# VectorE's exponential in three operations instead of four, and a table that decides which score banks it gets

## The chip, the cores and the metric

One core of one Trainium2 chip runs the kernel. The metric is the device time of one execution in microseconds; of several executions the median is given. Engines are called as the profile calls them: PE is TensorE's matmuls and PEld its weight loads, DVE is VectorE, ACT is ScalarE, POOL is GpSimd, SP is SyncE.

## The reference

Two transformer layers with shared weights, over S = 2048 rows of D = 448 values, 16 heads of 28, a hidden layer of 1792, all in bfloat16:

```
def A(x, wqkv, wo):                     # attention
    q, k, v = split(x @ wqkv)           # 16 heads of 28
    p = softmax(q @ k.T * 28 ** -0.5)
    return (p @ v) @ wo
def B(x, w1, b1, w2, b2):               # dense
    r = relu(x @ w1 + b1)
    return (r * r) @ w2 + b2
for layer in range(2):
    x = x + A(layernorm(x)); x = x + B(layernorm(x))
```

The softmax needs 2 x 16 x 2048 x 2048 exponentials: 1,048,576 for each of the 128 partitions. No maximum is subtracted; the sum of each row comes out of the product with the values, to which a column of ones is added.

## The kernel before

**A plan, not a loop.** The kernel issues its instructions in an order that a planner (class Planner, L145) works out while the program is built. Each piece of work is a generator ("stream") that yields Ops: an engine, a cost in us, what it depends on, what buffer it takes and gives back. The planner keeps a clock for each engine, always takes the Op that can start first, and among equals the stream with the smaller priority number. The engines then run their instructions in this order, so a change of any cost or rule orders all engines anew.

**Units, groups and banks.** The scores are cut into 2048 units, 1024 for each layer: one unit is 512 columns of scores, in one PSUM bank, for one head (128 keys by 256 queries, twice). s_stream (L865) lets PE compute the scores of three units into one of two PSUM buffers (`sc`, three banks each); this is a group, and there are 683. e_stream (L946) lets ACT take the exponential of a whole group in one instruction (L955) into an SBUF buffer `pt`. p_stream (L1054) multiplies the exponentials by the values (L1105). QK matmuls may be repeated to keep PE busy (L917 to L923), and heat (L1516) adds matmuls whose result nobody reads (L1531).

**Banks for DVE.** For each group s_stream asks `apart` (L821) whether DVE may take the third bank. If so, ACT's instruction covers two banks, 1024 columns, and DVE computes the third bank's exponential itself. `apart` says no in the first 15 groups and the last 60 units, when no scratch set is free (`sets_of`, two or three sets, each held from a unit's first operation to its last), when DVE's planned load over 11 us is above a limit, and by the test that the change touches: DVE's planned lead over PE's clock, plus `left`, the DVE time still to be planned for units already taken, must not be above TB = 2.2 us. If `behind(i)` (L805) says that the other work of the layer is behind a straight line, the limits are LOW = 0.95 of load and TB2 = 0.9 us instead. `done` (L802) counts that other work, at the end of each matmul tile of the output projection, the dense layers and the next layer's projections.

**DVE's exponential** (a_unit L1000 and a_rest L1021) has four operations on a bank of 128x512. The scores come as log2 of the exponential times 2^17. The first (L1011) reads PSUM, adds a bias, cuts off low values and writes int32: the upper 16 bits are the whole exponent, the lower 16 bits the fraction. The second (L1026, "power") reads the upper half as int16 and builds the bits of a power of two. The third (L1033, "square") computes (f + a) * f from the lower half f, as uint16. The fourth (L1041, "close") adds a constant, multiplies by the power and writes bfloat16. The first frees the score bank and has priority 1.6; the other three are a stream of their own with priority 8.5, which becomes 5.2 or 3.5 with age. The row work's evictions have 2.9 (EV), a row block's chain 4 to 4.8.

**Row work and its place.** Once a block of 256 rows has all its heads, `chain` (L1244) does output projection, layernorm, the two dense layers and, in layer 0, the keys, queries and values of layer 1 (L676, L672, L704). Its PSUM tiles are the two banks `mt`, and DVE evicts nearly all of them. Layer 1's scores begin with keys 0 to 9 (in tiles of 128 rows) for the first 13 passes and go on to keys 10 to 15 from unit 1284, so the keys of the last two row tiles of layer 0 are first needed at unit 1292.

Of the kernel before, what the change touches and what calls it, by code (L numbers as in the profile page):

```python
# [11 lines left out]
DT = mybir.dt  # L12
AF = mybir.ActivationFunctionType
ALU = mybir.AluOpType
P = 128
# [7 lines left out]

FRAC = 17
EXP_BIAS = -0.08179355555318127 * 2.0 ** FRAC
EXP_LOW = -56.0 * 2.0 ** FRAC
EXP_BASE = 91.0 * 2.0 ** 23 + 13573.0 * 2.0 ** 7
EXP_POLY = (4.803267716767392 * 2.0 ** 16, 14.031064225079138 * 2.0 ** 32)  # L30
OVER = 0.08
QUICK = 2
QUICK3 = 2
# [5 lines left out]
DCLK = 0.2  # L39
OWN = 2  # L40
HALF = 320
L0E = 1310
L0N = 7.2
L1E = 1900
L1N = 5.4
MARGIN = 1.5
LOW = 0.95
TURNS = 1
ENDU = 100
HOTE = 0.8  # L50
# [26 lines left out]
LEAD = 15  # L77
LAST = 690
BUSY = 0.995
TB = 2.2  # L80
TB2 = 0.9
SPAN = 11
NPT = 11
NOS = 2
# [154 lines left out]
def kernel(  # L239
# [12 lines left out]
    nc = tc.nc  # L252
# [16 lines left out]
    const = ctx.enter_context(tc.tile_pool(name="const", bufs=1))  # L269
# [13 lines left out]
    pl = Planner()  # L283
# [503 lines left out]
    units = []  # L787
# [11 lines left out]

    taken = set()  # L800
    held = [0]
    done = [0.0, 0.0]  # L802
    per = [1.6 + 7 + 5.6 + 6.0, 1.6 + 7 + 5.6]

    def behind(i):  # L805

        l = 0 if i < L0E else 1
        a, b, n = ((280, L0E, L0N), (1440, L1E, L1N))[l]
        return done[l] < (min(i, b) - a) / (b - a) * n * per[l] - MARGIN
    pending = [0]  # L810
    left = [0.0]

# [8 lines left out]
    def apart(i, now, us, soon=SOON):  # L821

        if len(units) - i < STOP or not LEAD <= len(gbuf) <= LAST:
            return None
        l, qb = passes[units[i][0]][:2]
        if sum(r.when() is not None and r.when() <= now + soon for r in sets_of(units[i])) <= (0 if soon else pending[0]):
            return None
        j = i
        if i + LAG > ends_at[units[i][0]]:
            j = ends_at[units[i][0]] + 1  # L830
            while j in taken:
                j += 1
            if j >= len(units):
                return None
            rows = {u[3] for u in us}
            js = [k for k in range(j, j + 4) if k < len(units) and k not in taken and units[k][3] not in rows]
            j = js[0] if js else j
        if passes[units[j][0]][0] != passes[us[0][0]][0]:
            return None
        if units[j][0] != us[0][0] and held[0] + 1 > min(sum(r.n for r in pd_free(units[k])) for k in (i, j)):  # L840
            return None
        if any(pl.tok.get(d) is None or pl.tok[d].end + LAT["DVE"] > now for d in needs(units[j])):
            return None
        if pl.load(SPAN, "DVE") > (LOW if behind(i) else BUSY):
            return None
        if max(0.0, pl.clock["DVE"] - now) + left[0] > (TB2 if behind(i) else TB):
            return None
        return j

# [116 lines left out]
    def pd_free(unit):  # L966

        pi, kb, r, hh = unit
        l, qb, *_ = passes[pi]
        if l == 0:  # L970
            return (R_pd[0], *(R_pd[1:5] if qb <= 6 else R_pd[3:5]))
        if len(norm_done.get((0, len(blocks[0]) - 1), ())) < G:
            return tuple(R_pd[:1])
        return tuple(R_pd[:1] + R_pd[6:]) if hidden_left[0] else tuple(R_pd[:1] + R_pd[5:])
# [8 lines left out]
            return V_sb[0][:, 8 + i, :, :].rearrange("p h r -> p (h r)")  # L983
        return hp.tile([P, QB], DT.bfloat16, name="h")[:, :]

    v_i = [const.tile([P, 512], DT.int32, name=f"v_i{k}") for k in range(2)]
    v_e = [const.tile([P, 512], DT.int32, name=f"v_e{k}") for k in range(2)]

    def set_of(res, l):

        k = R_v.index(res)
        two = lambda a: a.rearrange("p (a n) -> p a n", a=2)
        if k < 2:
            i, e = two(v_i[k][:, :]), two(v_e[k][:, :])
        else:
            keys = K_sb[1 - l][:, :, S - 512:S] if l == 0 else K_sb[0][:, :, 0:512]
            i, e = keys[:, 0:2, :].bitcast(DT.int32), keys[:, 2:4, :].bitcast(DT.int32)
        return i, e, i.bitcast(DT.float32), two

    def a_unit(gi, x, src, unit, l):  # L1000
        yield Op("-", 0.0, None, deps=[("s", gi)])
        box = {}

        def take(e):
            pending[0] -= 1
            box["i"], box["e"], box["h"], two = set_of(c.res, l)
            box["two"] = two
            halves = box["i"].bitcast(DT.uint16).rearrange("p a (n t) -> p a n t", t=2)
            box["f"] = halves[:, :, :, 0]
            box["n"] = box["i"].bitcast(DT.int16).rearrange("p a (n t) -> p a n t", t=2)[:, :, :, 1]  # L1010
            t = nc.vector.tensor_scalar(out=box["i"], in0=two(src), scalar1=EXP_BIAS,  # L1011
                                        scalar2=EXP_LOW, op0=ALU.add, op1=ALU.max)
            if x is gbuf[gi]["s"]:
                apart_from(gi, t)
        c = Op("DVE", 0.69, take, deps=[("s", gi)], acq=sets_of(unit), rel=x)
        left[0] += 2.14
        yield c
        left[0] -= 0.6
        pl.spawn(lambda now: V_LAST if e_now[1] - gi >= V_AGE or at[0] > ends_at[unit[0]] + V_PAST else V_LATE if now > c.end + V_WAIT else V_PRIO if gi > FIRST else V_FIRST, a_rest(gi, c, box, unit))

    def a_rest(gi, c, box, unit):  # L1021

        lin, low = EXP_POLY

        def power(e):
            nc.vector.tensor_scalar(out=box["e"], in0=box["n"], scalar1=2.0 ** 22, scalar2=EXP_BASE,  # L1026
                                    op0=ALU.mult, op1=ALU.add)
        p = Op("DVE", 0.42, power, deps=[c])
        yield p
        left[0] -= 0.34  # L1030

        def square(e):
            nc.vector.scalar_tensor_tensor(out=box["h"], in0=box["f"], scalar=lin, in1=box["f"],  # L1033
                                           op0=ALU.add, op1=ALU.mult)
        h = Op("DVE", 0.684, square, deps=[c, p])
        yield h
        left[0] -= 0.6

        def close(e):
            pd = gbuf[gi]["pd"] = gbuf[gi]["pt"][:, 1024:1536] if gbuf[gi]["in"] else pd_of(o)  # L1040
            nc.vector.scalar_tensor_tensor(out=box["two"](pd), in0=box["h"], scalar=low, in1=box["e"].bitcast(DT.float32),  # L1041
                                           op0=ALU.add, op1=ALU.mult)
        own = gbuf[gi]["in"]
        o = Op("DVE", 0.683, close, deps=[p, h, ("e", gi)] if own else [p, h], acq=None if own else lambda: pd_free(unit), rel=c, sets=("x", gi))
        gbuf[gi]["x"] = o
        yield o
        left[0] -= 0.6
# [196 lines left out]
    def chain(l, qb):  # L1244
# [3 lines left out]
        n = nt * P  # L1248
# [8 lines left out]
        for j in range(nt):  # L1257
            if whole:
                def both(e, t):
                    nc.vector.tensor_copy(out=x_sb[:, t0, :], in_=t[:, 0:D])  # L1260
                a = yield from mm_tile(
                    [(0, D, [(ident[:, :], x_sb[:, t0, :])] + [(oTn[:, g, 0:P], wo[:, g, :], *([("on", l, qb, g)] if end else [])) for g in range(G)])],
                    both, 0.61, [*([] if end else norm_done[l, qb]), *[("wo", i) for i in range(G)]],
                    alone=G if end else 0, seen=lambda last, t: stats(mv, t0, 0, [last], src=lambda: t()[:, 0:D]))
                done[l] += 0.8
                continue
            a = yield from mm_tile(
                [(0, D, [(oTn[:, g, j * P:(j + 1) * P], wo[:, g, :], *([("on", l, qb, g)] if end else [])) for g in range(G)])],
                add_to_x(t0 + j), 0.61, [*([] if end else norm_done[l, qb]), *[("wo", i) for i in range(G)]],
                post=[lambda a, j=j: stats(mv, t0, j, [a])], alone=G - 1 if end else 0)  # L1270
            done[l] += 0.8
        yield Op("DVE", 0.0, None, deps=[a], rel=own_on)
        xnT, own_xt, ends = yield from layernorm(t0, nt, None, mv=mv, x_in=a, parts=late > 2 - THALF)
        rows_done.add((l, qb))
# [15 lines left out]
        for f0 in range(0, NFC, pack):  # L1290
            fcs = range(f0, min(f0 + pack, NFC))
            w = len(fcs) * n
            split = late > 2 - THALF and f0 == 0
            b = {}
# [15 lines left out]
            def then(o, b=b, square=square):  # L1310
# [4 lines left out]
                [(i * n, n, [(w1[:, dc, fc * P:(fc + 1) * P], xnT[:, dc, 0:n], *([ends[dc // 2]] if split else [])) for dc in range(NDC)])  # L1315
                 for i, fc in enumerate(fcs)],
                relu, 0.685, [*([] if split else ends), ("w1",)], True, post=[then], acq=R_r, across=split)
            done[l] += w / 512
            for i in range(len(fcs)):
                hacts.append((b, i, b["s"]))  # L1320
        yield Op("DVE", 0.0, None, deps=[o], rel=own_xt)
# [1 line left out]
        for j in range(nt):  # L1323
            tb = t0 + j
            own_deps = l == 1 and qb >= len(blocks[1]) - OWN
            halves = [(0, D)] if not HALF or (l, qb) != (1, len(blocks[1]) - 1) else [(0, HALF), (HALF, D)]
            for lo, hi in halves:
                def store(e, tb=tb, lo=lo, hi=hi):
# [4 lines left out]
                    add_to_x(tb, lo, hi), 0.15 + (hi - lo) / 950, [*([] if own_deps else [hacts[-1][2]]), ("w2",), ("b2",)],  # L1333
                    post=[(lambda a, j=j: stats(mv, t0, j, [a])) if l == 0 else
                          (lambda a, store=store: [Op("DMA", 0.5, store, deps=[a])])])
            done[l] += 2.8
        yield Op("DVE", 0.0, None, deps=[a], rel=own_h)
        hidden_left[0] -= l == 0
        if l == 0:
            xt2 = yield from layernorm(t0, nt, None, mv=mv)  # L1340
            yield from qkv(1, t0, nt, *xt2)
            done[0] += 6.0

    def finish(l, qb):

# [237 lines left out]
```

## Time and profile before

| | us |
|---|---|
| median of 3 runs | 857.73 (856.56 to 859.1) |
| span of the profiled execution, first to last instruction | 854.4 |
| median less span | 3.3 |
| ACT busy | 838.1 (98%), of which exponentials 827.5 |
| PE busy | 812.8 (95%) |
| DVE busy | 809.8 (95%) |
| last exponential ends at | 840.0 |

The profiled execution is one execution, and the profile gives its span; no other time of it is recorded. The median of the timed runs is 3.3 us above that span. A line of instructions in the profile names line, engine, operation, output and inputs, shapes, how often, busy us in total, mean ns of one, and the engine's idle time ahead of it. Two instructions of one engine can overlap in the records, so that sums of durations may exceed the time they fill; the distance from one start to the next is then the better measure.

### The profile page before, as it was taken

The numbers are of one execution on the slowest core, as the hardware profiler recorded it, in microseconds if no ns is written. First come the engines' busy times: TensorE is split into PE (matmuls) and PEld (weight loads), VectorE is DVE, ScalarE is ACT, GpSimd is POOL, SyncE is SP. The second block draws the span as 40 slices with busy tenths as digits, with TensorE's granted clock in tenths as the row PEclk, the third lists the DMA queues.
The fourth block names the chain that finished last, engine by engine and source line by source line (L and its number), as shares of the span: only waits on it lengthen the run. The fifth ranks groups of instructions, "written<-read, shape, count | busy, mean of one in ns | idle before, by whom it ended". The sixth has DMA issues, their size and how long they took to land.

```text
span 854.4 us, 28129 instructions
## 1 busy us (share of the span) xinstructions
PE 812.8 (95%) x12245; PEld 431.4 (50%) x12245; DVE 809.8 (95%) x1687; ACT 838.1 (98%) x699; POOL 40.1 (5%) x94
## 2 busy tenths in 40 slices
PE   8999999999999999999999999999999999999997
PEld 4445554554545545455445444544454544545665
DVE  7999999999999999999999999999999999999965
ACT  8999999999999999999999999999999999999994
POOL 3100000001000010000000000000000000000000
PEclk9999999999999999999999999899999999999999
DMA  9200100000000000000000000011000000000000
GB/s 247 67 3 2 28 16 15 14 16 15 15 3 15 16 15 15 7 11 15 2 2 2 3 2 2 16 29 28 29 13 20 21 26 20 17 17 14 20 14 13
DMA packets 32364, 17.97 MB, mean 21 GB/s; under 512 B 17833, under 2 KB 31787, under 8 KB 32240
## 3 DMA queue, kind: packets, MB, share of 16 engines
q1 hardware_dynamic: 32240, 16.18, 6.8%
q8 instruction: 95, 1.56, 0.8%
q14 instruction: 29, 0.24, 0.1%
HBM read 13.88 MB, written 2.07 MB: 19 GB/s over the span
## 4 chain that ended last, share of the span: by engine, by line
PE 35%; ACT 32%; DVE 24%; issue 7%; DMA 0%; SPq 0%; POOL 0%; ACTq 0%; DVEq 0%
ACT pt L955 32%; PE mt L653 15%; PE sc L930 12%; PE oT L1105 6%; DVE v_i L1011 3%; DVE v_i L1033 3%; DVE pt L1041 2%; DVE r L1301 2%; DVE K_sb L1011 2%; DVE v_e L1026 2%; DVE K_sb L1033 1%; PE mt L1531 1%; DVE V_sb L1041 1%; DVE x_sb L1241 1%; DVE st L507 1%
## 5 line engine op out<-in xcount | busy, mean ns | idle before, releaser
L955 ACT ACTIVATE pt<-sc 128x1536 bf16<-128x1536 f32 (+1 forms) x683 | 827.5, 1446 | 2.5 <-PE sc L930 2.1
L930 PE MATMUL sc<-Q_sb,K_sb 32*128 32x256 bf16 (+1 forms) x5192 | 303.6, 266 | 28.3 <-ACT pt L955 24.0
L930 PEld LDWEIGHTS <-K_sb 32*128 32x128 bf16 x5192 | 128.5, 92 | 210.0 <-issue 163.2
L1105 PE MATMUL oT<-pt,V_sb 128*32 128x256 bf16 (+1 forms) x4084 | 152.5, 269 | 0.3 <-DVE Q_sb L672 0.2
L653 PE MATMUL mt<-xnT,w 128*128 128x256 bf16 (+1 forms) x888 | 118.9, 271 | 2.1 <-DVE xnT L569 0.7
L1105 PEld LDWEIGHTS <-V_sb 128*32 128x32 bf16 x4352 | 91.4, 96 | 46.5 <-issue 43.0
L1011 DVE TENSOR_SCALAR v_i<-sc 128x512 int32<-128x512 f32 x154 | 104.9, 681 | 5.6 <-PE sc L930 5.2
L1033 DVE SCALAR_TENSOR_TENSOR v_i<-v_i 128x512 f32<-128x512 uint16 x154 | 104.3, 679 | 0.5
L653 PEld LDWEIGHTS <-w 128*128 128x128 bf16 x896 | 75.0, 98 | 37.6 <-issue 28.3
L1301 DVE TENSOR_SCALAR r<-mt 128x512 bf16<-128x512 f32 x108 | 73.6, 681 | 3.8 <-PE mt L653 3.4
L653 PE MATMUL mt<-w,V_sb 128*128 128x448 bf16 (+1 forms) x288 | 70.0, 348 | 0.0
L1026 DVE TENSOR_SCALAR v_e<-v_i 128x512 int32<-128x512 int16 x154 | 62.8, 413 | 0.5
L1531 PE MATMUL mt<-xn,ident 128*128 128x448 bf16 x161 | 53.9, 358 | 2.0 <-DVE oT_sb L1133 0.4
L534 POOL TENSOR_TENSOR ve<-mv,eps_t 128x2 f32<-128x2 f32 (+1 forms) x33 | 9.4, 285 | 779.0 <-DVE mv L512 779.0
L1041 DVE SCALAR_TENSOR_TENSOR pt<-v_i,v_e 128x512 bf16<-128x512 f32 x63 | 42.9, 681 | 0.7
L1241 DVE TENSOR_TENSOR x_sb<-x_sb,mt 128x448 bf16<-128x448 bf16 x62 | 37.7, 610 | 5.5 <-PE mt L653 5.3
L1011 DVE TENSOR_SCALAR K_sb<-sc 128x512 int32<-128x512 f32 x60 | 41.0, 683 | 2.1 <-PE sc L930 1.9
L1033 DVE SCALAR_TENSOR_TENSOR K_sb<-K_sb 128x512 f32<-128x512 uint16 x60 | 40.8, 680 | 0.3
L507 DVE BATCH_NORM_STATS2 st<-x_sb 128x6 f32<-128x448 bf16 x63 | 38.7, 614 | 0.5 <-DMA x_sb<-in_A_x_dram 0.4
L1041 DVE SCALAR_TENSOR_TENSOR V_sb<-v_i,v_e 128x512 bf16<-128x512 f32 x54 | 36.7, 679 | 0.2
L653 PEld LDWEIGHTS <-V_sb 128*128 128x128 bf16 x302 | 24.1, 97 | 24.4 <-issue 11.4
L653 PE MATMUL mt<-wo,oTn 128*128 128x448 bf16 x124 | 30.7, 355 | 0.4 <-DVE oT_sb L1133 0.3
(135 smaller groups left out, 736.0 us busy)
## 6 DMA issues: line engine op xcount, KB each, us to landing
rec<-scr SPq DMA_DIRECT2D x54, 128.0 KB
x_sb<-in_A_x_dram SPq DMA_DIRECT2D x8, 224.0 KB
out_dram<-x_sb SPq DMA_DIRECT2D x15, 112.0 KB
w<-in_B_w_dram SPq DMA_DIRECT2D x1, 1568.0 KB
w<-in_B_w_dram SPq DMA_DIRECT2D x1, 1344.0 KB
dn<-oT_sb SPq DMA_DIRECT2D x54, 4.0 KB
V_sb<-in_A_wqkv_dram SPq DMA_DIRECT2D x4, 168.0 KB
scr<-dn SPq DMA_DIRECT2D x27, 8.0 KB
```

Of the source, the lines that this page charges most:

```text
L507: nc.vector.bn_stats(out=box["st"][:, :], in_=x_sb[:, t0 + j, :] if src is None else src())
L653: nc.tensor.matmul(box["t"][:, c0:c0 + n], lhsT=lhsT() if callable(lhsT) else lhsT, rhs=rhs, start=a, stop=b)
L930: nc.tensor.matmul(dst[k][:, i * nt * P:(i + 1) * nt * P], lhsT=K_sb[l][rows, g, (kb + i) * P:(kb + i + 1) * P], rhs=Q_sb[rows, g, t0 * P: ...
L955: t = nc.scalar.activation(out=pt[:, 0:n], in_=gbuf[gi]["sc"][:, 0:n], func=AF.Exp, scale=float(np.log(2.0)) * 2.0 ** -FRAC)
L1011: t = nc.vector.tensor_scalar(out=box["i"], in0=two(src), scalar1=EXP_BIAS, scalar2=EXP_LOW, op0=ALU.add, op1=ALU.max)
L1026: nc.vector.tensor_scalar(out=box["e"], in0=box["n"], scalar1=2.0 ** 22, scalar2=EXP_BASE, op0=ALU.mult, op1=ALU.add)
L1033: nc.vector.scalar_tensor_tensor(out=box["h"], in0=box["f"], scalar=lin, in1=box["f"], op0=ALU.add, op1=ALU.mult)
L1041: nc.vector.scalar_tensor_tensor(out=box["two"](pd), in0=box["h"], scalar=low, in1=box["e"].bitcast(DT.float32), op0=ALU.add, op1=ALU.mult)
L1105: nc.tensor.matmul(box["t"][DHP * hh:DHP * hh + DHP, 0:n], lhsT=V_sb[l][:, kb + i, 4 * g + hh, :], rhs=p[:, c0:c0 + n], start=begin and kb ...
L1241: nc.vector.tensor_tensor(out=x_sb[:, tb, lo:hi], in0=x_sb[:, tb, lo:hi], in1=t[:, 0:hi - lo], op=ALU.add)
L1301: nc.vector.tensor_scalar(out=r[:, 0:w], in0=t[:, 0:w], scalar1=0.0, scalar2=None, op0=ALU.max)
L1531: nc.tensor.matmul(t[:, 0:D], lhsT=ident[:, :], rhs=xns[0][:, 0:D], start=True, stop=True)
```

## The change

DVE's exponential gets three operations. Scores now come as log2 times 2^7. The first operation (tensor_scalar, PSUM to SBUF) writes float32 after an addition that puts the value where the low 16 bits of its float32 pattern hold the position within one octave. The second (scalar_tensor_tensor) reads these low halves as int16 and computes a bend, (f * c) * f, into a second float32 scratch tile. The third (scalar_tensor_tensor) adds value, constant and bend and writes the sum as int16 into the bfloat16 tile: the whole number is the bit pattern of the result. The operation "power" is gone; the scratch tile `v_e` (int32) becomes `v_h` (float32) of the same size. The planner's figure for a unit is 1.80 instead of 2.14 us.

The tests `behind`, LOW, TB and TB2 and the counting in `done` go. In their place stands PACE, 64 limits of 0.3 to 6.0 us; unit number i uses entry i * 64 // 2048, so each entry covers 32 units. The load limit is BUSY = 0.995 always.

```diff
-FRAC = 17
-EXP_BIAS = -0.08179355555318127 * 2.0 ** FRAC
-EXP_LOW = -56.0 * 2.0 ** FRAC
-EXP_BASE = 91.0 * 2.0 ** 23 + 13573.0 * 2.0 ** 7
-EXP_POLY = (4.803267716767392 * 2.0 ** 16, 14.031064225079138 * 2.0 ** 32)
+FRAC = 7
+EXP_MID = 0.506
+EXP_LOW = 128.0 * 128
+EXP_SHIFT = 184.0 * 128 - round(EXP_MID * 2.0 ** 16) / 512
+EXP_BEND = 0.3418455151161652 * 128 / 65536 ** 2
+EXP_BITS = (127.0 - 0.08538929525245402) * 128 - EXP_SHIFT
...
-TB = 2.2
-TB2 = 0.9
+PACE = (3.6, 3.6, 3.6, 1.8, 1.8, 1.8, 1.8, 1.8, 0.3, 0.9, 2.2, 2.2, 2.2, 2.6, 3.0, 3.0, 3.0, 3.6, 6.0, 2.2, 2.2, 2.2, 4.5, 2.2, 3.0, 2.6, 2.2, 2.2, 2.6, 2.6, 1.8, 1.8, 2.2, 2.6, 2.6, 1.8, 1.8, 1.8, 2.2, 2.6, 3.0, 6.0, 2.6, 4.5, 1.4, 1.4, 1.4, 1.4, 1.4, 1.4, 1.4, 1.4, 2.2, 2.2, 2.2, 2.2, 2.2, 2.2, 2.2, 2.2, 2.2, 2.2, 2.2, 2.2)
...
-        if pl.load(SPAN, "DVE") > (LOW if behind(i) else BUSY):
+        if pl.load(SPAN, "DVE") > BUSY:
             return None
-        if max(0.0, pl.clock["DVE"] - now) + left[0] > (TB2 if behind(i) else TB):
+        if max(0.0, pl.clock["DVE"] - now) + left[0] > PACE[i * len(PACE) // len(units)]:
             return None
...
-            halves = box["i"].bitcast(DT.uint16).rearrange("p a (n t) -> p a n t", t=2)
-            box["f"] = halves[:, :, :, 0]
-            box["n"] = box["i"].bitcast(DT.int16).rearrange("p a (n t) -> p a n t", t=2)[:, :, :, 1]
-            t = nc.vector.tensor_scalar(out=box["i"], in0=two(src), scalar1=EXP_BIAS,
+            box["f"] = box["i"].bitcast(DT.int16).rearrange("p a (n t) -> p a n t", t=2)[:, :, :, 0]
+            t = nc.vector.tensor_scalar(out=box["i"], in0=two(src), scalar1=EXP_SHIFT,
                                         scalar2=EXP_LOW, op0=ALU.add, op1=ALU.max)
...
-        left[0] += 2.14
+        left[0] += 1.80
...
-        def power(e):
-            nc.vector.tensor_scalar(out=box["e"], in0=box["n"], scalar1=2.0 ** 22, scalar2=EXP_BASE,
-                                    op0=ALU.mult, op1=ALU.add)
-        p = Op("DVE", 0.42, power, deps=[c])
-        yield p
-        left[0] -= 0.34
-
         def square(e):
-            nc.vector.scalar_tensor_tensor(out=box["h"], in0=box["f"], scalar=lin, in1=box["f"],
-                                           op0=ALU.add, op1=ALU.mult)
-        h = Op("DVE", 0.684, square, deps=[c, p])
+            nc.vector.scalar_tensor_tensor(out=box["h"], in0=box["f"], scalar=EXP_BEND, in1=box["f"],
+                                           op0=ALU.mult, op1=ALU.mult)
+        h = Op("DVE", 0.684, square, deps=[c])
...
-            nc.vector.scalar_tensor_tensor(out=box["two"](pd), in0=box["h"], scalar=low, in1=box["e"].bitcast(DT.float32),
-                                           op0=ALU.add, op1=ALU.mult)
+            nc.vector.scalar_tensor_tensor(out=box["two"](pd.bitcast(DT.int16)), in0=box["i"], scalar=EXP_BITS, in1=box["h"],
+                                           op0=ALU.add, op1=ALU.add)
```

## The prediction

> **What bounds the kernel now.** First the page's busy times: ACT 98%, PE and DVE 95% each. Three engines near the top say only that shares cannot decide. Second, what ACT waited for over the whole run:
>
> ```profile
> ACT pt L955 <- PE sc L930: 2.1, 5, 1.0
> ```
>
> Only 2.1 us of waiting for scores, in 5 places. Third, the same line with its two shapes kept apart, and busy times by stretch. The stretches run from the first bank that DVE takes (30.1 us) to the end of the last (807.5), and from the end of the last exponential (839.9) to the end of the span; the columns are the length, then busy time and count of PE, PEld, DVE, ACT and POOL, PE's granted clock, DMA share and GB/s:
>
> ```profile
> L955 ACT ACTIVATE pt<-sc 128x1536 bf16<-128x1536 f32 x468 | 668.7, 1581 | 1.8 <-PE sc L930 1.4
> L955 ACT ACTIVATE pt<-sc 128x1024 bf16<-128x1024 f32 x215 | 236.9, 1154 | 0.8 <-PE sc L930 0.7
> ...
> 30.10:807.50 777.40, 745.33 (x11094) 388.70 (x11092) 756.33 (x1538) 776.26 (x646) 29.25 (x67) 1.00 0.05 14
> ...
> 839.90:854.40 14.50, 10.76 (x133) 7.83 (x131) 7.54 (x26) 3.04 (x7) 0.56 (x1) 0.99 0.06 18
> ```
>
> ACT is busy 776.3 of 777.4 us: its exponentials stand end to end and set the time. 468 x 3 + 215 x 2 banks = 1834, and DVE's 214 make the 2048. DVE is idle 777.4 - 756.3 = 21.1 us of the stretch, so ACT cannot give it many more banks as things are. The kernel is bound by the two together: ACT by its exponentials, DVE by how many banks it can relieve ACT of.
>
> **What a bank is worth to ACT.** 1581 - 1154 = 427 ns. The records overlap, but the starts agree: the median distance from one exponential to the next is 1.331 us after three banks and 0.904 after two. The count of 683 instructions stays, since a group is always three units.
>
> **What a bank costs DVE now.** The four operations, in their most frequent forms:
>
> ```profile
> L1011 DVE TENSOR_SCALAR v_i<-sc 128x512 int32<-128x512 f32 x154 | 104.9, 681 | 5.6 <-PE sc L930 5.2
> L1033 DVE SCALAR_TENSOR_TENSOR v_i<-v_i 128x512 f32<-128x512 uint16 x154 | 104.3, 679 | 0.5
> ...
> L1026 DVE TENSOR_SCALAR v_e<-v_i 128x512 int32<-128x512 int16 x154 | 62.8, 413 | 0.5
> L1041 DVE SCALAR_TENSOR_TENSOR pt<-v_i,v_e 128x512 bf16<-128x512 f32 x63 | 42.9, 681 | 0.7
> ```
>
> Durations of 681 + 413 + 679 + 681 make 2.45 us, but the timeline (start, duration) shows that they are not the cost:
>
> ```profile
> 143.92 0.68 DVE L1033 SCALAR_TENSOR_TENSOR v_i<-v_i 128x512 f32<-128x512 uint16 x1
> 144.52 0.42 DVE L1026 TENSOR_SCALAR K_sb<-K_sb 128x512 int32<-128x512 int16 x1
> 144.86 0.68 DVE L1041 SCALAR_TENSOR_TENSOR pd<-v_i,v_e 128x512 bf16<-128x512 f32 x1
> 145.46 0.68 DVE L1033 SCALAR_TENSOR_TENSOR K_sb<-K_sb 128x512 f32<-128x512 uint16 x1
> ...
> 402.25 0.69 DVE L1033 SCALAR_TENSOR_TENSOR v_i<-v_i 128x512 f32<-128x512 uint16 x1
> 402.98 0.69 DVE L1041 SCALAR_TENSOR_TENSOR V_sb<-v_i,v_e 128x512 bf16<-128x512 f32 x1
> ```
>
> From start to start a long operation takes 0.60 us (144.86 to 145.46) and the power 0.34 (144.52 to 144.86). Where an operation needs the one just ahead of it, the slot grows by about 0.12 (402.25 to 402.98). A unit so takes 3 x 0.60 + 0.34 = 2.14 us.
>
> **What the change removes.** The power, 0.34 us for each unit: 214 x 0.34 = 73 us of DVE. The three that stay keep their size, and their slots should stay at 0.60. The first writes float32 instead of int32 from PSUM; L1301, which also reads a PSUM bank but writes bf16, has 681 ns as well, so the output type is not what counts. The square reads int16 instead of uint16 in the same places. The close reads two float32 tiles as before and writes int16 instead of bf16, two bytes either way. For these I take nothing; bounds from the rows are 0.34 (413 ns, the shortest operation on a bank of 512) and 0.60 + 0.12 us for each. Dependent pairs fall from three in a unit to two, and a filler between the first and the third operation goes; I take the two as equal. The change issues no DMA, adds no wait to another engine, and moves no queue but through the new plan.
>
> The Trainium skill, "VectorE: DVE Perf Modes", section "The DRAIN you can't avoid", says that the next operation does not start until the pipe of the one before is empty. Taken as a slot of the whole recorded duration, the power would be worth 0.413 us and all units 88 us, and the result by the sum below would be 842.4 before the idle time is touched; the timeline does not agree, with starts 0.08 us ahead of the recorded ends.
>
> **Where the freed time goes.** If the planner took no more banks, DVE would just idle and the time would stay, since ACT has the same work. What it takes more is decided by the tests in apart. All of them let DVE fill up: the load limit stays 0.995, the backlog test has 2.2 or more in 44 of 64 entries and counts 1.80 us for a unit instead of 2.14, and a scratch set is held for less time. So I set the balance with DVE as full as now. In the stretch, units fill 214 x 2.14 = 458.0 us; other work and idle time are 777.4 - 458.0 = 319.4. With n units the stretch is 777.4 - 0.427 (n - 214) on ACT and 319.4 + 1.80 n on DVE. Equal: 2.227 n = 549.4, n = 246.7. So 32.7 more banks, 14.0 us less. The idle 21.1 us is the other term: none of it to all of it can be filled, the latter giving n = 256.2 and 18.0 us; I take a third, because most of DVE's waits that the trace names are for PE's tiles, which stay. 7.0 us is 3.2 units and 1.3 us. **The sum is 14.0 + 1.3 = 15.3 us**, so the profiled execution of 854.4 becomes 839.1. The median lies 3.3 above that span; I keep that: 842.4.
>
> **What must hold beside it.** PE has the same useful work in 15 us less. It is busy 745.3 of 777.4, but that holds filling: L930 ran 5192 matmuls where 2048 units need 4352 (layer 1's last two blocks need four per unit), and L1531 ran 161 with 53.9 us that nobody reads. The cover is several times 15 us; gone, each us of PE would count in full. The granted clock dips once, and ACT does not notice:
>
> ```profile
> 534.00:560.70 26.70, 25.47 (x385) 12.96 (x384) 25.41 (x52) 26.43 (x24) 0.00 (x0) 0.87 0.06 13
> ```
>
> Start (10.8 us) and tail (14.5) have no bank for DVE and stay.
>
> **Rival 1: the rows of layer 0 come too late, slower.** Layer 1's scores need the last keys of layer 0's rows at unit 1292, about the 431st group, whose exponential starts near 533 us. The timeline has these keys written just in time:
>
> ```profile
> 530.24 0.68 DVE L676 CAST K_sb<-mt 128x512 bf16<-128x512 f32 x1
> 530.84 0.68 DVE L1011 TENSOR_SCALAR v_i<-sc 128x512 int32<-128x512 f32 x1
> ...
> 538.16 0.68 DVE L676 CAST K_sb<-mt 128x512 bf16<-128x512 f32 x1
> ```
>
> The progress test that held DVE for the rows (0.9 us when behind) is gone, and the table's entries ahead of that unit are 1.8 to 2.6. A bank taken there beyond the balance pushes the rows back 1.80 us and spares 0.43, a net loss of 1.37. 135 units were taken by 531 us, so 21 of the 33 new ones belong there; 14.0 / 1.37 = 10 further ones eat the gain, and 12 make it slower by 0.3%. With 15 it is 20.6 lost, 863. For it: no slack at 530 us. Against: only the first operation has a priority ahead of the rows (1.6), the other two wait at 8.5 behind evictions at 2.9. Chance 0.09.
>
> **Rival 2: score banks come free late, slower.** With more units in flight DVE's first operation may end after ACT's and hold the buffer. To lose 15.3 + 2.6 us, 250 units must each delay ACT by 72 ns; I put it at 862. Now in 206 of 214 cases the first operation ends ahead of ACT's own exponential of that group, in the median by 0.45 us. Chance 0.03.
>
> **Rival 3: the freed time is not refilled.** The table is tight (0.3 and 0.9 for units 256 to 319, 1.4 for 1408 to 1663), or a scratch set is the limit: it is held 6.0 us in the mean, 214 x 6.0 / 777 = 1.65 sets of two or three. Nothing gained is 857.7, chance 0.06 within 0.3%; a part of it, 6 to 20 banks, is 849 to 855, chance 0.12.
>
> **More than forecast:** all idle time and all 0.12 us gaps filled adds to 20.5 us, 837; below that 0.02.
>
> **How the numbers follow.** Forecast 842.4 with 837 to 849 around it: 0.68. A measurement tells about 0.3%, 2.6 us, from no change. Faster by more: 0.68 + 0.12 + 0.02 = 0.82. Same: 0.06. Slower: 0.09 + 0.03 = 0.12. The range 837 to 854 leaves out rivals 1 and 2, the standstill and a little at either end, some 0.2.
>
> **What would show it.** About 250 first and last operations on DVE and about 250 exponentials of 128x1024; slots still 0.60; ACT's wait for scores a few us; the last exponential near 825. Wrong if the count of 128x1024 stays at 215 to 225, if ACT's idle time grows around the keys of layer 0's last rows, or if a scalar_tensor_tensor with int16 in or out takes longer than 0.68 us.

## The result and the profile after

| | before | after |
|---|---|---|
| median, us | 857.29 (856.56 to 859.10, 4 runs) | 848.77 (848.31 to 848.86, 4 runs) |
| span of the profiled execution | 854.4 | 847.0 |
| ratio of the times, 95% interval | | 0.990 (0.9886 to 0.9914) |
| banks on DVE | 214 | 244 |
| first exponential starts, last one ends | 10.85, 839.96 | 10.66, 832.54 |
| last exponential's end to end of span | 14.4 | 14.4 |

The change makes the kernel 1.0% faster: 8.5 us by the medians, 7.4 by the two profiled spans. (The median before has one run more than ahead of the prediction, hence 857.29 in place of 857.73.) The forecast was 842.4, a gain of 15.3. The time lies in the range; the gain is a little over half of the forecast by the medians and a little under half by the spans.

The groups of the kernel after show what became of the four operations and of ACT's instruction (count, then busy us and mean ns of one):

```profile
L941 ACT ACTIVATE pt<-sc 128x1536 bf16<-128x1536 f32 x438 | 628.4, 1566 | 4.0 <-PE sc L916 3.6
L941 ACT ACTIVATE pt<-sc 128x1024 bf16<-128x1024 f32 x245 | 263.6, 1143 | 2.8 <-PE sc L916 2.6
```

The DVE groups of the kernel after, first operation, square and close:

```profile
L995 DVE TENSOR_SCALAR v_i<-sc 128x512 f32<-128x512 f32 x175 | 119.1, 682 | 6.9 <-PE sc L916 6.1
L1008 DVE SCALAR_TENSOR_TENSOR v_h<-v_i 128x512 f32<-128x512 int16 x175 | 117.5, 679 | 0.5
...
L995 DVE TENSOR_SCALAR K_sb<-sc 128x512 f32<-128x512 f32 x69 | 47.1, 683 | 3.1 <-PE sc L916 2.4
...
L1016 DVE SCALAR_TENSOR_TENSOR pt<-v_i,v_h 128x512 int16<-128x512 f32 x64 | 43.0, 672 | 0.3
```

The three operations cost what their forerunners did, 672 to 683 ns, with int16 in or out; from one start to the next each has a median of 0.60 us, as before. 175 + 69 = 244 units went to DVE, 30 more, and the three-bank exponentials fell from 468 to 438. That alone is worth 30 x 0.427 = 12.8 us. ACT's waits in the kernel after show where a part of it went:

```profile
ACT pt L941 <- PE sc L916: 6.2, 11, 2.2
```

6.2 us where it was 2.1. Measured from start to start, against 1.331 us after three banks and 0.904 after two, ACT's excess over back-to-back is 17.1 us; before it was 11.4. The spans add up: 0.2 from an earlier start, 12.8 from the banks, 5.7 given back, the tail the same: 7.3 of the 7.4.

Two places hold most of the 5.7, 4.8 together. Between 30 and 110 us the excess rose from 1.05 to 4.12, between 545 and 560 us from 0.97 to 2.69. The first is a row-work deadline of layer 0: its last keys (row tiles 12 to 15) are first needed at units 160 and 164. ACT in the kernel after around it (start, duration, and the idle time ahead in brackets):

```profile
74.36 4.91 ACT L941 ACTIVATE pt<-sc 128x1536 bf16<-128x1536 f32 x4
81.51 1.02 ACT L941 ACTIVATE pt<-sc 128x1024 bf16<-128x1024 f32 x1 [2.24 <-PE sc L916]
```

DVE in the same stretch of the kernel after:

```profile
77.54 0.68 DVE L1008 SCALAR_TENSOR_TENSOR v_h<-v_i 128x512 f32<-128x512 int16 x1
78.14 0.68 DVE L563 COPY xnT<-tp 128x1024 bf16<-128x1024 bf16 x1
78.74 0.68 DVE L1016 SCALAR_TENSOR_TENSOR V_sb<-v_i,v_h 128x512 int16<-128x512 f32 x1
79.34 0.41 DVE L1108 TENSOR_TENSOR K_sb<-oT,K_sb 128x256 f32<-128x256 f32 x1
79.67 0.68 DVE L1008 SCALAR_TENSOR_TENSOR v_h<-v_i 128x512 f32<-128x512 int16 x1
80.27 0.68 DVE L670 CAST K_sb<-mt 128x512 bf16<-128x512 f32 x1
```

ACT stands still for 2.24 us because the scores wait for the keys that L670 writes at 80.27; DVE has no gap, and three of the five operations ahead belong to banks that it took (L1008, L1016). The same keys were written earlier in the kernel before:

```profile
76.66 0.69 DVE L676 CAST K_sb<-mt 128x512 bf16<-128x512 f32 x1 [0.47 <-PE mt L653]
```

The keys of the same rows for the other heads follow at 86 us with 0.8 us more. The second place is a stretch of half granted clock, taken up under fill.

DVE's stretch in the kernel after, with the columns of the prediction's table:

```profile
30.10:800.00 769.90, 741.43 (x11094) 388.06 (x11095) 739.47 (x1413) 764.14 (x646) 30.82 (x66) 0.99 0.05 14
```

DVE's idle time there is 769.9 - 739.5 = 30.4 us; it was 21.1. So DVE was not filled further, as the forecast assumed, but a little less.

### The profile page after: what moved, and what is told of

It reads as the page before. It is cut to its first block, busy times and chain, and to the rows that moved or that the text cites. A ratio compares the mean times of both kernels' runs of the same rounds, so it can differ in the third digit from the quotient of the medians.

```text
span 847.0 us, 27977 instructions
## 1 busy us (share of the span) xinstructions
PE 809.2 (96%) x12200; PEld 430.6 (51%) x12200; DVE 793.7 (94%) x1563; ACT 826.4 (98%) x699; POOL 41.7 (5%) x94
## 4 chain that ended last, share of the span: by engine, by line
PE 48%; ACT 27%; DVE 15%; issue 7%; DMA 2%; POOL 1%; ACTq 0%; SPq 0%; DVEq 0%
ACT pt L941 27%; PE mt L647 20%; PE sc L916 16%; PE oT L1080 8%; DVE v_i L995 2%; DVE v_h L1008 2%; PE mt L1501 2%; DVE r L1274 1%; DVE pt L1016 1%; DVE K_sb L1008 1%; DVE K_sb L995 1%; DVE st L501 1%; DVE x_sb L1216 1%; DMA rec<-scr 1%; DVE xn L611 1%
## 5 line engine op out<-in xcount | busy, mean ns | idle before, releaser
L941 ACT ACTIVATE pt<-sc 128x1536 bf16<-128x1536 f32 (+1 forms) x683 | 815.7, 1415 | 6.8 <-PE sc L916 6.2
L916 PE MATMUL sc<-Q_sb,K_sb 32*128 32x256 bf16 (+1 forms) x5180 | 306.8, 267 | 27.6 <-ACT pt L941 21.5
L916 PEld LDWEIGHTS <-K_sb 32*128 32x128 bf16 x5180 | 131.6, 92 | 205.9 <-issue 153.1
L1080 PE MATMUL oT<-pt,V_sb 128*32 128x256 bf16 (+1 forms) x4034 | 154.5, 270 | 0.7 <-DVE pt L1016 0.3
L995 DVE TENSOR_SCALAR v_i<-sc 128x512 f32<-128x512 f32 x175 | 119.1, 682 | 6.9 <-PE sc L916 6.1
L1008 DVE SCALAR_TENSOR_TENSOR v_h<-v_i 128x512 f32<-128x512 int16 x175 | 117.5, 679 | 0.5
L1080 PEld LDWEIGHTS <-V_sb 128*32 128x32 bf16 x4352 | 90.9, 96 | 50.0 <-issue 46.9
L1274 DVE TENSOR_SCALAR r<-mt 128x512 bf16<-128x512 f32 x108 | 73.4, 680 | 4.7 <-PE mt L647 4.4
L995 DVE TENSOR_SCALAR K_sb<-sc 128x512 f32<-128x512 f32 x69 | 47.1, 683 | 3.1 <-PE sc L916 2.4
L1008 DVE SCALAR_TENSOR_TENSOR K_sb<-K_sb 128x512 f32<-128x512 int16 x69 | 46.8, 678 | 0.3
L1216 DVE TENSOR_TENSOR x_sb<-x_sb,mt 128x448 bf16<-128x448 bf16 x62 | 37.6, 611 | 7.3 <-PE mt L647 6.8
L1501 PE MATMUL mt<-xn,ident 128*128 128x448 bf16 x128 | 44.1, 357 | 0.3
L1016 DVE SCALAR_TENSOR_TENSOR pt<-v_i,v_h 128x512 int16<-128x512 f32 x64 | 43.0, 672 | 0.3
L1016 DVE SCALAR_TENSOR_TENSOR V_sb<-v_i,v_h 128x512 int16<-128x512 f32 x63 | 42.5, 678 | 0.2
L647 PEld LDWEIGHTS <-wk 128*128 128x128 bf16 x256 | 22.2, 97 | 11.4 <-issue 8.3
```

Of the source, the lines that this page charges most:

```text
L647: nc.tensor.matmul(box["t"][:, c0:c0 + n], lhsT=lhsT() if callable(lhsT) else lhsT, rhs=rhs, start=a, stop=b)
L916: nc.tensor.matmul(dst[k][:, i * nt * P:(i + 1) * nt * P], lhsT=K_sb[l][rows, g, (kb + i) * P:(kb + i + 1) * P], rhs=Q_sb[rows, g, t0 * P: ...
L941: t = nc.scalar.activation(out=pt[:, 0:n], in_=gbuf[gi]["sc"][:, 0:n], func=AF.Exp, scale=float(np.log(2.0)) * 2.0 ** -FRAC)
L1016: nc.vector.scalar_tensor_tensor(out=box["two"](pd.bitcast(DT.int16)), in0=box["i"], scalar=EXP_BITS, in1=box["h"], op0=ALU.add, op1=ALU.add)
L1080: nc.tensor.matmul(box["t"][DHP * hh:DHP * hh + DHP, 0:n], lhsT=V_sb[l][:, kb + i, 4 * g + hh, :], rhs=p[:, c0:c0 + n], start=begin and kb ...
L1216: nc.vector.tensor_tensor(out=x_sb[:, tb, lo:hi], in0=x_sb[:, tb, lo:hi], in1=t[:, 0:hi - lo], op=ALU.add)
```

## The experiments

Theory 1: ACT's exponentials stand end to end and set the time; a bank on DVE is worth 0.427 us of it, and each wait of ACT for scores counts in full. Cheaper banks let DVE take more, but the table's part is that keys are written by the time they fall due. Theory 2, the rival: DVE is the bound, and what is saved for each bank shows whatever the order. Times are medians, with the ratio to the kernel before on the same chip and its 95% interval.

**ops_only**: the new operations with the old limits.

```diff
-        if pl.load(SPAN, "DVE") > BUSY:
+        if pl.load(SPAN, "DVE") > (LOW if behind(i) else BUSY):
...
-        if max(0.0, pl.clock["DVE"] - now) + left[0] > PACE[i * len(PACE) // len(units)]:
+        if max(0.0, pl.clock["DVE"] - now) + left[0] > (TB2 if behind(i) else TB):
```

> The three operations with the old limits (behind, LOW, TB, TB2) in place of the table. Theory 1 (ScalarE's exponentials stand end to end and set the time; a bank given to VectorE is worth 0.427 us, and every wait of ScalarE for scores counts in full; the table's part is that the last keys of a layer are written before their scores are due): the planner's own order here has 243 banks on VectorE, so 29 x 0.427 = 12.4 us less of exponentials than before, but a wait for scores of some 7 us at the keys of layer 0's last rows (unit 1292, near 525 us) and of some 3 us near 78 us, and more work left after the last exponential: 856 to 862, no gain. Theory 2 (VectorE is the bound, so its time saved per bank shows whatever the order): 847 to 851, like the changed kernel.

Measured: 862.05, ratio 1.0058 (1.0039 to 1.0078), 243 banks. With one bank fewer than the changed kernel it is 0.6% slower than before. ACT at the due keys in ops_only:

```profile
525.10 3.84 ACT L956 ACTIVATE pt<-sc 128x1024 bf16<-128x1024 f32 x3
536.79 5.54 ACT L956 ACTIVATE pt<-sc 128x1024 bf16<-128x1024 f32 x5 [7.85 <-PE sc L931]
```

DVE's cast of these keys in ops_only:

```profile
535.00 0.69 DVE L677 CAST K_sb<-mt 128x512 bf16<-128x512 f32 x1 [1.96 <-PE mt L654]
```

The keys due near 527 us came at 535.0, and ACT waited 7.85 us. The time after the last exponential grew too, to 18.8 us. The time is at the upper edge of theory 1's range and 11 us above that of theory 2.

**table_only**: the four operations with the table (the same two lines the other way round, in the kernel before).

> The four operations of before with the table in place of the old limits. Theory 1: 213 banks, so the same exponentials as before, plus waits of some 5 us at unit 1292 that the old limits did not have: 861 to 867, slower than before. Theory 2: VectorE's work is that of before, 855 to 859. A table that is good by itself: below 855.

Measured: 869.63, 1.0144 (1.0116 to 1.0173), 213 banks; the wait at the due keys is 6.2 us. It lies 2.6 us above the range of theory 1: other waits came on top (12.2 us in all), with a half clock of 20.5 us after 556 us. The table is no gain by itself.

**cap214**: the changed kernel, banks held to the old number.

```diff
+        if len(taken) >= (i - 45) * 214 / 1945:
+            return None
```

> The changed kernel, but the number of banks for VectorE is held to a straight line that ends at 214, as many as before. Theory 1: VectorE's freed time is idle, ScalarE has the exponentials of before: 855 to 861, no gain although every bank costs VectorE less. Theory 2: 214 x 0.34 = 73 us less of VectorE's work show at least in part: below 852.

Measured: 858.75, 1.0017 (1.0005 to 1.0029). The stretch of before, 30.1 to 807.5 us (length, then PE, PEld, DVE, ACT, POOL), in cap214:

```profile
30.10:807.50 777.40, 745.15 (x11180) 395.37 (x11181) 702.95 (x1324) 774.75 (x645) 31.81 (x66) 1.00 0.05 14
```

DVE is busy 703.0 us where it was 756.3, and the time is that of before within 0.3%. 53 us taken from an engine that is 97% busy bought nothing, as long as no bank moved. (53 and not 73: an operation that nothing follows at once counts with its whole 0.68 instead of 0.60, and DVE's gaps rose from 138 to 321, which is worth some 15 us of the 20.)

**flat22**: all 64 entries 2.2.

```diff
-PACE = (3.6, 3.6, 3.6, 1.8, ...
+PACE = (2.2,) * 64
```

> The changed kernel with all 64 entries of the table 2.2, the old general limit, and nothing that looks at progress. Theory 1: 242 banks (12.0 us less of exponentials), but the rows of layer 0 come late: a wait of some 7 us near 525 us, one of some 10 us close to the end, and the 3 us near 78 us: 864 to 870, slower than before with 28 more banks on VectorE. Theory 2: 847 to 851.

Measured: 868.69, 1.0151 (1.0124 to 1.0177), 242 banks. ACT at the due keys in flat22:

```profile
537.05 4.40 ACT L941 ACTIVATE pt<-sc 128x1024 bf16<-128x1024 f32 x4 [8.49 <-PE sc L916]
```

There are three long waits of ACT, near the places that theory 1 named: 2.6 us near 79 us by the starts, 8.5 at the due keys and 9.1 near 833 us. The last is not a wait for keys: ACT waits there until PE has multiplied earlier exponentials by the values (L1080), behind matmuls of the dense layers. 28 more banks than before, and 1.5% slower.

**flat22_hold**: flat22 with five entries changed.

```diff
-PACE = (2.2,) * 64
+PACE = (2.2,) * 36 + (0.3,) * 5 + (2.2,) * 23
```

> The table is 2.2 everywhere, as in flat22, but its entries 36 to 40 (units 1152 to 1311, about 470 to 537 us, just ahead of and around the unit that needs the last keys of layer 0's rows) are 0.3. Theory 1 (what matters is that the rows' keys are written in time): 239 banks, three fewer than flat22, and yet 852 to 858, some 12 us faster than flat22's 868.7, with no wait of ScalarE over 1 us between 500 and 545 us. Theory 2 (more banks, more gain): flat22's time or 1 us more, 868 to 871.

Measured: 858.22, 1.0005 (0.9993 to 1.0017), 239 banks. By the medians it is 10.5 us faster than flat22, with three banks fewer. The casts of the last keys in flat22_hold:

```profile
525.12 0.68 DVE L670 CAST K_sb<-mt 128x512 bf16<-128x512 f32 x1
532.28 0.68 DVE L670 CAST K_sb<-mt 128x512 bf16<-128x512 f32 x1
```

They come in time, and there is no wait over 1 us there. The time is 0.2 us above theory 1's range. Its span is 9.4 us longer than the changed kernel's: 4.1 at the end (18.5 us after the last exponential instead of 14.4), 2.1 from five banks fewer, and 3.4 from more excess of ACT, of which 2.1 fall between 541 and 562 us, where the clock is halved for 20.5 us.

**keys_earlier**: the same work, the keys due 20 units earlier.

```diff
-AHEAD = (range(0, 4), range(0, 4), range(0, 4), range(0, 1))
+AHEAD = (range(0, 4), range(0, 4), range(0, 4), range(0, 0))
```

> The changed kernel with its table, but layer 1's first cut has 12 passes instead of 13 (AHEAD's last entry empty), so that the last keys of layer 0's rows are needed 20 units, some 8 us, earlier; the amount of work is the same. Theory 1: 248 banks, four more, but a wait of 5 to 8 us near 520 us where the changed kernel has none, and a longer end: 855 to 861. Theory 2: 846 to 849.

Measured: 860.28, 1.0039 (1.0024 to 1.0054), 248 banks. ACT in keys_earlier:

```profile
514.80 6.12 ACT L941 ACTIVATE pt<-sc 128x1536 bf16<-128x1536 f32 x5
528.22 1.94 ACT L941 ACTIVATE pt<-sc 128x1024 bf16<-128x1024 f32 x2 [7.30 <-PE sc L916]
```

DVE's cast of the due keys, first in keys_earlier, then in the changed kernel:

```profile
526.12 0.69 DVE L670 CAST K_sb<-mt 128x512 bf16<-128x512 f32 x1 [1.96 <-PE mt L647]
...
526.90 0.69 DVE L670 CAST K_sb<-mt 128x512 bf16<-128x512 f32 x1 [1.19 <-PE mt L647]
```

The keys are written at almost the same time; the due date moved by 8 us, and a wait of 7.3 us comes where there was none. In the changed kernel the keys end at 527.6 us and ACT's exponential that needs them starts at 528.2: they have next to no room.

**no_load_limit**: the limit on DVE's planned load lifted.

```diff
-BUSY = 0.995
+BUSY = 9.0
```

> The changed kernel without the limit of 0.995 on VectorE's planned load over 11 us (set to 9). Theory 1: 259 banks, 15 more, 6.4 us less of exponentials, but there is no room for them: the last keys of layer 0's rows come some 25 us late and the end is longer: 872 to 882, the slowest with the most banks. Theory 2: 840 to 845.

Measured: 881.14, 1.0292 (1.0271 to 1.0313). The two shapes of the exponential in no_load_limit:

```profile
L941 ACT ACTIVATE pt<-sc 128x1536 bf16<-128x1536 f32 x423 | 616.8, 1583 | 3.4 <-PE sc L916 2.9
L941 ACT ACTIVATE pt<-sc 128x1024 bf16<-128x1024 f32 x260 | 287.0, 1148 | 33.7 <-PE sc L916 33.5
```

ACT at the due keys in no_load_limit:

```profile
524.92 2.98 ACT L941 ACTIVATE pt<-sc 128x1536 bf16<-128x1536 f32 x2
552.70 1.94 ACT L941 ACTIVATE pt<-sc 128x1024 bf16<-128x1024 f32 x2 [24.80 <-PE sc L916]
```

259 banks, the least exponential time of all, and the slowest kernel. This also shows that with this table it is the load limit that keeps the number of banks at 244. With that limit, the kernels with three operations have 237 to 248 banks with every table tried here, cap214 aside.

**late_start**: DVE's first bank at group 40.

```diff
-LEAD = 15
+LEAD = 40
```

> The changed kernel, but VectorE gets its first bank at group 40 instead of 15 (LEAD), so that the opening's keys are not behind it. Theory 1: 237 banks, 7 fewer, 3.0 us more of exponentials; the wait of 3.4 us at 78 and 86 us is gone; the sum is 847 to 850, the same as the changed kernel's 848.8. Theory 2: 3 us slower, 851 to 853.

Measured: 850.14, 0.992 (0.9903 to 0.9937), 237 banks. No wait near 79 us is left, and the span of the profiled execution, 847.5, equals that of the changed kernel within 0.5 us with seven banks fewer. The median is just above the range of theory 1; two of the four runs had more half clock.

**fill**: more for PE around 548 us, where the clock is halved.

```diff
-                for i in list(range(4)) * (again + 1):
+                for i in list(range(4)) * (again + 1 + (438 <= gi < 462)):
```

> The changed kernel in the same order, but the score matmuls of groups 438 to 461 (about 540 to 565 us) are issued once more, so that TensorE does more there. In the changed kernel the granted clock is 0.5 for 10.2 us from 547.9 us, and ScalarE's excess over back-to-back between 545 and 560 us is 2.7 us. Theory A (TensorE does too little just ahead, the clock falls, and the scores then come late): the stretch of 0.5 gets shorter or goes, the excess there falls below 1 us, 846 to 848. Theory B (the waits there come from the order of the work, the clock has no part): the excess stays or grows by the added matmuls, 849 to 851.

Measured: 854.54, 0.9968 (0.9953 to 0.9984), from 850.3 to 857.4: slower than the changed kernel and above the ranges of both theories. The half clock did not go; it scattered. Sorted by mean granted clock, the spans of the 12 runs are 848.5 at 1.000, 850.1 to 850.2 at 0.996, 852.6 to 852.8 at 0.992, 854.2 to 854.3 at 0.990 and 855.5 to 855.6 at 0.988. So the time goes with the clock, some 1.2 us of span for each 3.4 us of half clock. But the added matmuls cost by themselves: the run at 1.000 is 1.5 us longer than the changed kernel's 847.0 at 0.994. And they kept the clock up in only one run of the 12.

**late_start2**: first bank at group 35, and one entry of the table.

```diff
-LEAD = 15
+LEAD = 35
...
-PACE = (..., 2.6, 2.6, 1.8, 1.8, 2.2, ...     # entries 28 to 32
+PACE = (..., 2.6, 2.6, 4.5, 1.8, 2.2, ...
```

> The changed kernel with VectorE's first bank at group 35 instead of 15, and entry 30 of the table (units 960 to 991) 4.5 instead of 1.8. Theory 1: 239 banks, 5 fewer, 2.1 us more of exponentials; the wait of 3.4 us of the opening is gone, all else as in the changed kernel: 847 to 848.5, about 1 us faster than it. Theory 2: 2 us slower, 850 to 852.

Measured: 847.61, 0.989 (0.9875 to 0.9905), 239 banks. Its waits for scores:

```profile
ACT pt L941 <- PE sc L916: 3.1, 8, 0.6
```

The opening's wait is gone, for 2.1 us more of exponentials. It has the lowest time of all, by 1.2 us in the medians; its interval overlaps that of the changed kernel (0.9886 to 0.9914), so that it is better is not shown.

**both**: late_start2 with the matmuls of fill.

> late_start2 with the added matmuls of fill. Theory 1 with theory A: both gains, 845 to 847.5. If the clock has no part: as late_start2, 847 to 850.

Measured: 850.82, 0.9936 (0.9916 to 0.9957), above the ranges of both theories. Here the profiled execution has no half clock in the stretch. Busy times and clock from 520 to 560 us in late_start2, which has the same order without the added matmuls (length, PE, PEld, DVE, ACT, POOL, clock, DMA share, GB/s):

```profile
520.00:560.00 40.00, 37.90 (x555) 19.76 (x554) 35.67 (x67) 38.36 (x34) 0.97 (x3) 0.87 0.07 17
```

The same stretch in both:

```profile
520.00:560.00 40.00, 38.32 (x668) 22.39 (x667) 35.49 (x67) 38.35 (x33) 0.86 (x3) 1.00 0.07 17
```

ACT is busy 38.4 of 40 us in each: here a full clock with added matmuls leaves as much waiting as 10.2 us of half clock without them. Over the 12 runs of both the span is 846.3 to 846.6 at a clock of 1.000 and 854.0 to 854.5 at 0.988. Whether the dip could be kept away without that price stays open.

## Why the prediction was right or wrong

**What bounds the kernel** was right. cap214 shows it for DVE: 53 us cheaper, no bank moved, no gain. For ACT it is the sum of the spans above, which comes out within 0.1 us from the count of banks and ACT's waits. PE's condition held too: in the kernel after, filling is left, with 5180 matmuls in L916 where 4352 are needed and 44.1 us in L1501 that nobody reads.

**The value of a bank, 0.427 us,** and **its cost on DVE, three slots of 0.60 us**, held, and int16 in or out cost nothing more, as taken. A slot of the whole recorded duration, which the prediction sets beside this, did not come; the passage of the Trainium skill that it cites for it ("VectorE: DVE Perf Modes", section "The DRAIN you can't avoid") itself adds that a next operation that is not held starts earlier.

**The balance** was a little high: 247 banks with DVE as full as before, 250 with a third of its idle time filled. It came to 244, with 9 us more idle. The step that failed is the one that took "a third, because most of DVE's waits that the trace names are for PE's tiles, which stay". They grew: DVE's waits that end with PE went from 13.5 to 22.3 us in its stretch. 6 banks fewer are 2.5 us of the 7.9 us by which the span missed. (The prediction lets the stretch before end with DVE's last bank at 807.5 us; that bank ends at 816.2, but DVE is not idle in between, so the 21.1 us stay.)

**The waits of ACT** are the larger miss. The forecast had no term for them: it expected "a few us" as before, and the 5.7 us more are the rest. Rival 1 had the place and the sign: ops_only, flat22, keys_earlier and no_load_limit wait 7.3 to 24.8 us for the keys that it named. But it was priced as a mishap at one place, and it showed at a second one where scores need keys that DVE evicts: at layer 0's own keys (units 160 to 180) the changed kernel pays 3.4 us of it by the starts. "Start and tail have no bank for DVE and stay" was true of the groups ahead of DVE's first bank and hid this. Its arithmetic, that 15 banks beyond the balance ahead of the due keys lose 20.6 us net, was too mild: no_load_limit has 15 more than after, 10 of them ahead of these keys, and is 32 us slower. Nor is it the number of banks alone. By 510 us DVE has begun 147 banks in the changed kernel, and 147 in flat22 and ops_only as well. Yet of the eleven results of the dense layers that DVE evicts between 440 and 530 us (L1274 in after and flat22, L1291 in ops_only), the changed kernel has ten out by 490 us, the other two eight, and the addition behind them (L1216, L1231) starts at 510.6 us against 521.9 and 522.3. So the table acts through where the row work falls in the order; why the planner puts it later without the table stays open.

**The chance of rival 1** was set too low for the wrong reason. The text held against it that DVE's second and third operations have a low priority. Yet the new operations lose to it with the old progress test (ops_only), which was thought to guard against it, and with a flat limit. The fitted table avoids it, and so does the flat limit with five entries held back (flat22_hold).

**Rival 2** did not come: in 227 of 244 groups DVE's first operation still ends ahead of ACT's. (Its condition alone gives 857.7 + 2.6 = 860.3, not 862.) **Rival 3** did not either: 30 banks moved.

**The clock**: the forecast said that ACT does not notice the dip. The excess at 545 to 560 us was 0.97 us before, with 6.8 us of half clock, and is 2.69 after, with 10.2; and over the runs of fill and both the span grows with the half clock, by 1.2 to 1.3 us for each 3.4 us of it. How much of the 1.7 us the clock makes and how much the order is not shown.

**Median over span**: 3.3 us was too much. For the runs after it is 1.8, and so it is for runs of before taken with the experiments (856.09 for a span of 854.3). The profiled execution of before was a short one among its runs. That is luck: the surplus, 1.5 us too high, hid a part of the 7.9 us by which the span missed, and so the median misses by 6.4.

## What to carry to other kernels

When two engines share work in a statically ordered kernel, a cheaper operation on the helper is worth only the work that then moves to it, counted on the engine that bounds; with nothing moved it is worth nothing. Before counting the moved work as gain, list each place where the bounding engine consumes what the helper also produces, with the slack that the trace shows there: a micro-second of lateness there undoes more than two moved banks. And a limit fitted to one order need not carry over to another: the same table gained 1.0% with three operations and lost 1.4% with four.

## What the runs showed of the hardware that was not expected

TensorE's granted clock was halved for stretches of 3.41, 6.83, 10.24, 13.65 and 20.48 us, all multiples of 3.413 us, in kernels that keep PE busy by the profile more than 90% of the time. The Trainium skill, "TensorE: Matmul & The Clock Gate", section "Part 1: The HAM clock gate (the "warmup" mystery)", says that a monitor sets the clock by the activity in a window of about 3.4 us; the lengths agree. In the kernels before and after and in most of the others a stretch begins between 541 and 557 us. In the kernel after it does so at 547.9, between the last queries of layer 0's rows (542.6) and the first row work of layer 1 (553.4). Why there is not shown: PE's longest gap between 520 and 560 us is 0.52 us in that kernel, and by the profile PE is busy all through the 3.4 us ahead. Other stretches do follow a gap: in flat22, ops_only, keys_earlier and no_load_limit, where scores wait long for the due keys, PE has a gap of 3.0 to 3.1 us, and the clock falls 2.6 to 4.1 us after it begins. The length of the half clock goes with most of the scatter between runs of one kernel: in both, spans of 846.5, 848.9, 851.2 and 854.3 us went with clocks of 1.000, 0.996, 0.992 and 0.988.
